# Opening the second matmul earlier, splitting its tiles in the first quads, and moving stores on a saturated TensorE

## The chip, the cores and the metric

The kernel runs on one core of one Trainium2 chip. The metric is the device time of one execution in microseconds (us), median of several runs. Before the change it was 341.34 us (three runs: 341.34, 342.12 and 340.13).

## What is computed

A forgetting attention (causal, with a decay from a cumulative sum of log f) over 8 batches, 8 heads, 576 positions and 64 dimensions is followed by a dense layer with SiLU, whose input row is the 8 heads' outputs side by side (512 wide), for 4608 rows:

```python
scores = scale * np.matmul(q, k.transpose(0, 1, 3, 2))
log_f = np.log(np.clip(f, 0.0001, 1.0))
cum = np.cumsum(log_f, axis=-1)
decay = cum[:, :, :, None] - cum[:, :, None, :]
scores = np.where(causal, -1000000000.0, scores + decay)
...
attn = attn / (np.sum(attn, axis=-1, keepdims=True) + 1e-09)
return np.matmul(attn, v).astype(np.float32)
...
x = np.ascontiguousarray(attn_out.transpose(0, 2, 1, 3)).reshape(B * S, H * D)
h = x @ w_in                          # 512 -> 2048
g = h * (1.0 / (1.0 + np.exp(-h)))
return (g @ w_out).astype(np.float32) # 2048 -> 512
```

## The kernel before

**The work.** The program is written out by hand; each engine and each DMA queue does its instructions in exactly the order in which the program lists them. Four kinds of TensorE work are interleaved.

- *Block 0 of each batch* (the first 128 positions of all heads): `turn0` (line 286, transposes q and k on TensorE, tile `tp`), `scores0` (line 318), `out0` (line 358, tile `dn`) and `back0` (line 391, transposes the result, tile `tx`; ScalarE copies it into the layer's input `x`, line 399). `two_more(b)` (line 857) does this for batches b and b+1, with pieces of the dense layer between the steps.
- *Units*: the other 448 positions of two heads are a unit n; four units are a batch, two units are a *quad* m, so there are 32 units and 16 quads (loop from line 960). For each unit `scores` (line 454) makes three pieces on TensorE, with the 64-row contraction of one head on each half of the array, and ScalarE takes the exponential (lines 474 and 480). `mask` and `mask_tail` (lines 484 and 490) zero the upper triangle on VectorE. `attend` (line 500) multiplies by the values (tile `dn`, lines 516 and 525) and VectorE divides (lines 533 and 534). `back(m)` (line 541) transposes a quad's result into `x`: for quads 0 to 2 and 15 on TensorE (tile `tx`, line 558, with VectorE's copies at lines 561 and 564), afterwards by DMA.
- *M1 chunks* (`m1_chunk`, line 570): 128 of the 2048 hidden columns for a group of rows (512, 256 or 384 wide), four matmuls into a tile `hp`; ScalarE makes `th` (line 585), VectorE makes `gt` (line 586).
- *M2 parts* (`m2_part`, line 604): a quarter of a 128-row output tile, four matmuls into `po`. After the fourth part ScalarE moves `po` to `osb` (line 632), and a store is put on a list. In quads 4 to 15 one M2 tile per quad is made in another way (`m2_rows`, line 639): the 128-row contraction is cut into halves of 64 rows that run side by side on the two halves of the array, 32 matmuls in each of two halves of the tile, into two tiles `pr`; VectorE moves them (`m2_fence`, `m2_out`, lines 657 and 661).

**The order.** `fill(us)` (line 748) lays down M1 chunks and M2 parts worth so many planned us; `step` (line 706) chooses between them; M2 may only run once `open2["w"]` is set (line 879, after the first `two_more` and a further `fill`). `whole` (line 913) finishes a started M2 tile and names the next whole one, if there is one. In a quad without a whole tile the order is the one from line 1004 on: pieces of the dense layer (`slot`) between the score pieces, then both `attend`. In a quad with one (line 981) the two halves of the M2 tile stand between the score pieces, and M1 chunks or M2 parts stand between the two `attend`.

**Buffers.** The PSUM tiles `tp`, `dn`, `tx`, `hp`, `po` and `pr` share four buffers (`pbig`, line 69); the score tiles have two of their own (`psc`, line 68). `osb` has four buffers (line 64), and `qkb`, the unit's q and k in bfloat16, has six (line 58).

**The supply.** SyncE's queue (SP) issues, in order: the loads of a unit's q (`qf`, line 167), of a batch's last positions (`qktf`, line 177) and of the values (`vf`, line 188), the DMA transposes of q and k (`qkT`, line 437), the stores (line 601) and the transposes of `back`. GpSimd (POOL) casts q (lines 410 and 414), issues the loads of k (line 158) and scales the values of a batch (`vp`, line 423, four instructions a batch). Unit n+3 is cast and transposed and unit n+4 is loaded in `turn(n)` (line 888); the values of batch 1 are loaded in `turn(2)` and `turn(3)` and needed first in unit 4, that is in quad 2. `store(n)` (line 598) issues the first n stores of the list; `slot` issues those that were on the list before it began.

Of the kernel before, what the change touches and what calls it, by code (L numbers as in the profile page):

```python
# [18 lines left out]
def kernel(  # L19
# [35 lines left out]

    const = ctx.enter_context(tc.tile_pool(name="const", bufs=1))
    stage = ctx.enter_context(tc.tile_pool(name="stage", bufs=1))
    conv = ctx.enter_context(tc.tile_pool(name="conv", bufs=6))
    qktp = ctx.enter_context(tc.tile_pool(name="qktp", bufs=4))
    upool = ctx.enter_context(tc.tile_pool(name="upool", bufs=4))  # L60
    recp = ctx.enter_context(tc.tile_pool(name="recp", bufs=2))
    xqp = ctx.enter_context(tc.tile_pool(name="xqp", bufs=2))
    tpool = ctx.enter_context(tc.tile_pool(name="tpool", bufs=3))
    opool = ctx.enter_context(tc.tile_pool(name="opool", bufs=4))
    xpool = ctx.enter_context(tc.tile_pool(name="xpool", bufs=1))
    setup_pool = tc.tile_pool(name="setup", bufs=1)
    setup = setup_pool.__enter__()
# [323 lines left out]
    def back0(b, *copies):  # L391
        xq = xqs.pop(b)[:, :, :].rearrange("p (c j) d -> p c (j d)", j=2)
        g, c0 = HEADS_OF[b]
        k = NCC // len(copies)
        for n, copy in enumerate(copies):
            tx = pbig.tile([P, k, P], BF16, name="tx", tag="big")
            for cc in range(k):
                nc.tensor.transpose(tx[:, cc, :], xq[:, n * k + cc, :], ident_bf[:, :])
            copy(out=xg(g)[:, n * k : (n + 1) * k, c0 : c0 + P], in_=tx[:, :, :])  # L399
# [100 lines left out]
    def attend(n):  # L500
        b, p = divmod(n, NP)
        if p % 2 == 0:
            xqs[n // 2] = xqp.tile([P, NGR, 2, D], BF16, name="xr", tag="xr", bufs=3)
        xq = xqs[n // 2]
        u, ut = us.pop(n), uts[n % 4]
        dn = pbig.tile([P, NGR, D + 1], FP32, name="dn", tag="big")

        def vals(kb, i):
            h = head(p, i)
            return v0[b][:, h, :] if kb == 0 else vbf[b][:, kb - 1, h, :]  # L510

        for i in range(2):
            for c in range(1, NM):
                for kb in range(c + 1):
                    o = AT[c, kb]
                    nc.tensor.matmul(  # L516
                        dn[:, i * NR + c - 1, :],
                        lhsT=u[:, i, o : o + P],
                        rhs=vals(kb, i),
                        start=(kb == 0),  # L520
                        stop=(kb == c),
                    )
        for i in range(2):
            for kb in range(NM + 1):
                nc.tensor.matmul(  # L525
                    dn[:, NGR - 1, :],
                    lhsT=ut[:, kb, i : i + 2, :].rearrange("p i t -> p (i t)"),
                    rhs=vals(kb, i),
                    start=(i == 0 and kb == 0),
                    stop=(i == 1 and kb == NM),  # L530
                )
        rec = recp.tile([P, NGR], FP32, name="rec", tag="rec")
        nc.vector.reciprocal(out=rec[:, :], in_=dn[:, :, D])
        nc.vector.tensor_tensor(  # L534
            out=xq[:, :, p % 2, :],
            in0=dn[:, :, 0:D],
            in1=rec[:, :, None].to_broadcast([P, NGR, D]),
            op=ALU.mult,
        )
# [166 lines left out]
    def step(force=0):  # L706

        a, c = at["m1"], at["m2"]
        want = wanted(a, c)
        if not want:  # L710
            return None
        g1 = M1[a][0] if a < len(M1) else NG
        g2 = M2[c][0] if c < len(M2) else NG
        can1 = g1 in ready and not (M1[a][1] == 0 and g1 > g2 + lag["g"])
        can2 = open2["w"] and c < len(M2) and g2 < g1
        kind = force if (force == 1 and can1) or (force == 2 and can2) else want
        if kind == 1:
            if M1[a][1] == 0:
                begin[g1] = (0, c)
            m1_chunk(g1, M1[a][1])  # L720
            at["m1"] += 1
            t = 4 * (GW[g1] / 2.4 + 2.5)
        else:
            m2_part(*M2[c])
            at["m2"] += 1
            t = 4 * (DM / 2.4 + 2.5)
        return t
# [20 lines left out]
    def fill(us_, least=0, ends=(0, 0)):  # L748

        left = us_ + at["left"]  # L750
        kinds = plan(left)
        kinds += [0] * (least - len(kinds))
        if any(ends) and kinds:
            if 2 not in kinds:
                kinds[0] = 2
            n1, n2 = len(kinds) - kinds.count(2), kinds.count(2)
            e0 = 1 if ends[0] else 0
            e1 = 1 if ends[1] and n2 > e0 else 0
            inner = n2 - e0 - e1
            n = n1 + inner  # L760
            mid = [2 if (x + 1) * inner // n > x * inner // n else 1 for x in range(n)]
            if inner and mid[-1] == 2 and e1 and not e0:
                mid = mid[::-1]
            kinds = [2] * e0 + mid + [2] * e1
        for k in kinds:
            t = step(k)
            if t is None:
                at["left"] = 0.0
                return
            left -= t / 1000  # L770
        at["left"] = left
# [85 lines left out]
    def two_more(b):  # L857
        for x in range(2):
            turn0(b + x, 0)
            turn0(b + x, 1)  # L860
        fill(1.2, 2)
        for x in range(2):
            scores0(b + x)
            mask0(b + x)
        fill(2.6 if b == 4 else 3.4, 3)
        out0(b)
        fill(0.6, 1)
        out0(b + 1)
        fill(0.8, 2)
        back0(b, on_act)  # L870
        fill(0.6, 1)
        back0(b + 1, on_act)
        fill(0.6, 1)

    fill(5.9)
    two_more(4)
    ready.add(1)
    fill(3.0)
    open2["w"] = True
    begin[M1[at["m1"]][0]] = (M1[at["m1"]][1], at["m2"])  # L880
    fill(6.0)
    two_more(6)
# [30 lines left out]
    def whole():  # L913

        while at["m2"] < len(M2) and M2[at["m2"]][2] and wanted(at["m1"], at["m2"]):
            t = step(2)
            at["left"] -= t / 1000
        c = at["m2"]
        while M1[at["m1"]][0] in ready and M1[at["m1"]][1] >= NFC - 4 and M2[c][0] == M1[at["m1"]][0]:
            at["left"] -= step(1) / 1000  # L920
        a = at["m1"]
        if c >= len(M2) or M2[c][2]:
            return None
        g1 = M1[a][0] if a < len(M1) else NG
        return M2[c][:2] if M2[c][0] < g1 else None
# [22 lines left out]
    def passed():  # L948
        for x in pending:
            x[0] -= 1  # L950
        while pending and pending[0][0] == 0:
            ready.update(pending.pop(0)[1])

    def slot(us_, least=0, ends=(0, 0)):
        n = len(stores)
        fill(us_, least, ends)
        store(n)
        passed()

    for m in range(NQ):  # L960
        n = 2 * m
        piece = 1.7 if m < 2 else 2.4
        if m == 2:
            assert at["m2"] >= M2_OF[0]
            first_pool.__exit__(None, None, None)
            gpools[0] = ctx.enter_context(tc.tile_pool(name="third", bufs=1))
            lag["g"] = 2
        if m == 4:
            lag["parts"] = 12
        goal = (spent() if m <= 4 else goal) + QUAD[m]  # L970
        rows = whole() if m > 0 and BY_DMA[m - 1] else None
        scores(n, 0)
        scores(n, 1)
        if m > 0:
            back(m - 1)
        turn(n)
        if m > 0:
            if m % 2 == 0:
                b = m // 2 - 1
                pending.append([2, [REST_OF[b]] + ([TAILS_OF[b][0]] if b == NM - 1 else [])])  # L980
        if rows:
            at["m2"] += 4
            m2_rows(*rows, 0)
            m2_fence(*rows)
            mask(n)
            scores(n, 2)
            scores(n + 1, 0)
            turn(n + 1)
            m2_rows(*rows, 1)
            mask_tail(n)  # L990
            mask(n + 1)
            scores(n + 1, 1)
            scores(n + 1, 2)
            m2_out(*rows)
            passed()
            attend(n)
            mask_tail(n + 1)
            slot(1.9, 3)
            attend(n + 1)
            slot(1.8)  # L1000
            rest(goal)
            at["left"] = 0.0
            continue
        slot(piece, 0, (1, 0))
        mask(n)
        scores(n, 2)
        scores(n + 1, 0)
        turn(n + 1)
        slot(piece, 0, (1, 0))
        mask_tail(n)  # L1010
        mask(n + 1)
        scores(n + 1, 1)
        scores(n + 1, 2)
        mask_tail(n + 1)
        slot(piece, 0, (1, 0))
        attend(n)
        attend(n + 1)
        slot(min(3.5, max(0.8, behind() - LAG)) if m > 1 else 0.8)
# [40 lines left out]
```

## Time and profile before

| What | Value |
|---|---|
| median of three runs | 341.34 us |
| the profiled execution, its own time | 340.98 us |
| its span, first to last instruction | 339.2 us |
| TensorE matmuls: `hp` line 577, 704 instructions | 122.1 us busy |
| `po` line 622, 400 instructions | 93.8 us busy |
| `pr` line 648, 768 instructions | 46.0 us busy |
| ScalarE: exponential of 128x1024 / `th` of 128x384 / `th` of 128x256, one | 1027 / 492 / 389 ns |
| VectorE: `gt` of 128x384 / `gt` of 128x256, one | 553 / 419 ns |
| VectorE: `osb` from `pr`, 128x256, one | 414 ns |
| DMA, mean over the span | 142 GB/s |

All times are microseconds from the start of the span unless marked ns. A busy TensorE is not TensorE at its peak: the profile models a matmul's end, so the time that a block of matmuls costs is read from the start of its first matmul to the start of the next block. A line of the timeline has the start, the time until the last instruction of the line ends, the engine, the line of code, the operation, the tiles and a count; in square brackets stands how long the engine was idle before it and what ended that.

Read from starts to starts in this way, four matmuls of an M2 part take 0.863 us, an M1 chunk 0.436 us (256 wide) or 0.650 us (384 wide), half an M2 tile in 64-row halves 1.75 us, and the attention product of one unit 0.85 us.

### The profile page before, as it was taken

The numbers are of one execution on the slowest core, as the hardware profiler recorded it, in microseconds if no ns is written. First come the engines' busy times: TensorE is split into PE (matmuls) and PEld (weight loads), VectorE is DVE, ScalarE is ACT, GpSimd is POOL, SyncE is SP. The second block draws the span as 40 slices with busy tenths as digits, with TensorE's granted clock in tenths as the row PEclk, the third lists the DMA queues.
The fourth block names the chain that finished last, engine by engine and source line by source line (L and its number), as shares of the span: only waits on it lengthen the run. The fifth ranks groups of instructions, "written<-read, shape, count | busy, mean of one in ns | idle before, by whom it ended". The sixth has DMA issues, their size and how long they took to land.

```text
span 339.2 us, 10025 instructions
## 1 busy us (share of the span) xinstructions
PE 330.6 (97%) x4132; PEld 222.4 (66%) x4132; DVE 193.6 (57%) x425; ACT 216.9 (64%) x389; POOL 137.4 (41%) x217
## 2 busy tenths in 40 slices
PE   7999899999999999999999999999999999999995
PEld 3745565577656768857766896867776676555654
DVE  4668935267567556655656865684672558334330
ACT  5766635677867767848748784875776485444431
POOL 8895417636756455454374434536060000000000
PEclk9999999999999999999999999999999999999999
DMA  8999999999999799999998969989763210001012
GB/s 151 190 185 222 182 210 155 199 236 177 156 190 236 117 215 134 163 211 151 168 178 172 142 130 175 134 168 165 148 123 66 56 37 33 31 33 64 33 62 63
DMA packets 144702, 48.00 MB, mean 142 GB/s; under 512 B 133328, under 2 KB 139728, under 8 KB 144656
## 3 DMA queue, kind: packets, MB, share of 16 engines
q1 hardware_dynamic: 115088, 36.60, 59.5%
q0 software_dynamic: 29408, 10.62, 26.6%
q8 instruction: 32, 0.52, 0.7%
q10 hardware_dynamic: 160, 0.13, 0.2%
q14 instruction: 14, 0.11, 0.1%
HBM read 36.85 MB, written 9.44 MB: 136 GB/s over the span
## 4 chain that ended last, share of the span: by engine, by line
PE 92%; ACT 2%; DVE 2%; DMA 2%; issue 1%; POOL 0%; POOLq 0%
PE hp L577 35%; PE po L622 24%; PE pr L648 12%; PE sc L469 7%; PE dn L516 6%; PE dn L525 3%; PE tp L294 2%; DMA qkb<-in_k_dram 2%; DVE u L344 1%; DVE gt L586 1%; ACT x L399 1%; PE sc L309 1%; PE sc L328 1%; ACT u L335 1%; PE tx L558 0%
## 5 line engine op out<-in xcount | busy, mean ns | idle before, releaser
L585 ACT ACTIVATE th<-hp 128x384 bf16<-128x384 f32 (+2 forms) x208 | 96.0, 469 | 78.7 <-PE hp L577 75.8
L586 DVE SCALAR_TENSOR_TENSOR gt<-th,hp 128x384 bf16<-128x384 bf16 (+2 forms) x208 | 107.1, 522 | 67.3 <-ACT th L585 58.5
L577 PE MATMUL hp<-x,w_in_bf 128*128 128x384 bf16 (+2 forms) x704 | 122.1, 321 | 1.5 <-ACT x L399 0.9
L577 PEld LDWEIGHTS <-w_in_bf 128*128 128x128 bf16 x832 | 79.4, 98 | 50.6 <-issue 1.8
L622 PE MATMUL po<-w_out_bf,gt 128*128 128x512 bf16 (+1 forms) x400 | 93.8, 371 | 0.0
L480 ACT ACTIVATE u<-sc 128x1024 bf16<-128x1024 f32 (+1 forms) x96 | 74.4, 814 | 6.4 <-PE sc L469 6.4
L622 PEld LDWEIGHTS <-gt 128*128 128x128 bf16 x400 | 37.6, 98 | 32.5 <-issue 0.2
L410 POOL CAST qkb<-qf 128x384 bf16<-128x384 f32 x32 | 16.7, 522 | 95.1 <-DMA qf<-in_q_dram 94.8
L648 PE MATMUL pr<-w_out_bf,gt 64*128 64x256 bf16 x768 | 46.0, 269 | 0.0
L158 POOL DMA_DIRECT2D qkb<-in_k_dram x56 | 43.8, 784 | 0.7 <-issue 0.7
L648 PEld LDWEIGHTS <-gt 64*128 64x128 bf16 x768 | 38.5, 94 | 2.8
L423 POOL TENSOR_TENSOR vp<-vf,w_bf 128x520 bf16<-128x520 f32 (+1 forms) x32 | 34.1, 1069 | 10.3 <-DMA vf<-in_v_dram 9.0
L632 ACT ACTIVATE osb<-po 128x512 f32<-128x512 f32 (+1 forms) x25 | 14.6, 583 | 22.6 <-PE po L622 19.5
L469 PE MATMUL sc<-qkT 64*128 64x128 bf16 (+1 forms) x640 | 27.9, 206 | 0.4 <-ACT u L480 0.3
L469 PEld LDWEIGHTS <-qkT 64*128 64x128 bf16 x640 | 19.9, 94 | 8.6 <-issue 6.5
L486 DVE TENSOR_TENSOR u<-u,tri 128x768 bf16<-128x768 bf16 x32 | 19.4, 605 | 10.5 <-ACT u L480 10.5
L474 ACT ACTIVATE ut<-sc 128x640 bf16<-128x640 f32 x32 | 22.5, 702 | 1.7 <-PE sc L469 1.3
L516 PEld LDWEIGHTS <-u 128*128 128x128 bf16 x576 | 20.6, 98 | 2.9
L516 PE MATMUL dn<-vp,u 128*128 128x65 bf16 x384 | 21.8, 194 | 0.0
L534 DVE TENSOR_TENSOR xr<-dn,rec 128x448 bf16<-128x448 f32 x32 | 20.0, 624 | 1.1
L516 PE MATMUL dn<-v,u 128*128 128x65 bf16 x192 | 20.0, 194 | 0.0
L577 PE MATMUL hp<-xt,w_in_bf 128*128 128x256 bf16 x128 | 16.6, 273 | 0.0
(72 smaller groups left out, 228.1 us busy)
## 6 DMA issues: line engine op xcount, KB each, us to landing
out_dram<-osb SPq DMA_DIRECT2D x32, 256.0 KB, 3.5
vf<-in_v_dram SPq DMA_DIRECT2D x26, 256.0 KB, 5.5
qf<-in_q_dram SPq DMA_DIRECT2D x64, 96.0 KB, 3.4
qkb<-in_k_dram POOLq DMA_DIRECT2D x56, 48.0 KB, 4.6
w_in_bf<-in_moe_w_in_dram POOLq DMA_DIRECT2D x4, 512.0 KB, 6.8
w_out_bf<-in_moe_w_out_dram POOLq DMA_DIRECT2D x4, 512.0 KB, 8.7
vf<-in_v_dram POOLq DMA_DIRECT2D x6, 256.0 KB, 10.3
qkb<-in_q_dram POOLq DMA_DIRECT2D x8, 128.0 KB, 5.5
```

Source lines behind the costliest of these rows:

```text
L158: nc.gpsimd.dma_start(out=t2[:, NR + 1 : NX, j * D : (j + 1) * D], in_=k[b, head(p, j), P:SM, :].rearrange("(c p) d -> p c d", p=P),)
L423: nc.gpsimd.tensor_tensor(out=vbf[b][r, c, :, :], in0=vst[b][c][r, :, :], in1=w_bf[r, c + 1, b * H : (b + 1) * H, None].to_broadcast([n, H ...
L469: nc.tensor.matmul(sc[:, i, o : o + q1 - q0], lhsT=kt, rhs=t[r, q0:q1], start=True, stop=True)
L474: nc.scalar.activation(out=ut[:, :, 0:3:2, :].rearrange("p k i t -> p i k t"), in_=sc[:, :, T0 : T0 + (NM + 1) * ST].rearrange("p i (k t) ...
L480: nc.scalar.activation(out=u[:, :, c * SM : c * SM + w], in_=sc[:, :, 0:w], func=ACT.Exp, scale=scale)
L516: nc.tensor.matmul(dn[:, i * NR + c - 1, :], lhsT=u[:, i, o : o + P], rhs=vals(kb, i), start=(kb == 0), stop=(kb == c),)
L534: nc.vector.tensor_tensor(out=xq[:, :, p % 2, :], in0=dn[:, :, 0:D], in1=rec[:, :, None].to_broadcast([P, NGR, D]), op=ALU.mult,)
L577: nc.tensor.matmul(hp[:, :], lhsT=w_in_bf[:, cc, fc * P : (fc + 1) * P], rhs=xcols(g, cc), start=(cc == 0), stop=(cc == NCC - 1),)
L585: nc.scalar.activation(out=th[:, :], in_=hp[:, :], func=ACT.Tanh, scale=0.5)
L586: nc.vector.scalar_tensor_tensor(out=gt[:, fc, :], in0=th[:, :], scalar=1.0, in1=hp[:, :], op0=ALU.add, op1=ALU.mult,)
L622: nc.tensor.matmul(po[:, :], lhsT=gt[:, fc, tb * P : (tb + 1) * P], rhs=w_out_bf[:, fc, m0:m1], start=(fc == 0), stop=(fc == NFC - 1),)
L648: nc.tensor.matmul(pos[g, tb][y], lhsT=gt[r, fc, tb * P : (tb + 1) * P], rhs=w_out_bf[r, fc, y * DM // 2 : (y + 1) * DM // 2], start=(half ...
```

## The change

Three things change, and the fill sizes around them.

1. M2 may run from the last `fill` of the first `two_more` on, one `fill` before what was there.
2. `whole()` is asked in every quad, so that quads 0, 1 and 2 run one M2 tile in 64-row halves (quad 3 finds no whole tile and keeps the old order). In quads 1 and 2 the transposes of `back(m - 1)` move from the head of the quad to behind the first `attend`. In quads 0 and 1 four M1 chunks stand between the two `attend` (`ones(4)`) and at least two behind them.
3. In quads 0 to 3 all stores on the list are issued at the head of the quad, ahead of the quad's loads on SP. `osb` gets a fifth buffer, and `qkb` gives up its sixth.

```diff
-    conv = ctx.enter_context(tc.tile_pool(name="conv", bufs=6))
+    conv = ctx.enter_context(tc.tile_pool(name="conv", bufs=5))
...
-    opool = ctx.enter_context(tc.tile_pool(name="opool", bufs=4))
+    opool = ctx.enter_context(tc.tile_pool(name="opool", bufs=5))
...
         back0(b + 1, on_act)
+        open2["w"] = True
         fill(0.6, 1)
...
     fill(3.0)
-    open2["w"] = True
...
+    def ones(k):
+        n = len(stores)
+        for _ in range(k):
+            step(1)
+        at["left"] = 0.0
+        store(n)
+        passed()
+
...
-        piece = 1.7 if m < 2 else 2.4
+        piece = 2.1 if m == 0 else 1.7 if m < 2 else 2.4
...
-        rows = whole() if m > 0 and BY_DMA[m - 1] else None
+        rows = whole()
+        late = bool(rows) and m > 0 and not BY_DMA[m - 1]
+        if m < 4:
+            store(len(stores))
         scores(n, 0)
         scores(n, 1)
-        if m > 0:
+        if m > 0 and not late:
             back(m - 1)
...
             mask_tail(n + 1)
-            slot(1.9, 3)
+            if late:
+                back(m - 1)
+            if m < 2:
+                ones(4)
+            else:
+                slot(1.9, 3)
             attend(n + 1)
+            if m < 4:
+                if m < 2:
+                    ones(2)
+                else:
+                    slot(min(5.3, max(0.8, behind() - LAG)))
+                continue
             slot(1.8)
```

The dense layer's work by quad, as the two programs list it (M1 chunks with their width, M2 parts, M2 tiles in halves):

| Quad | Before | After |
|---|---|---|
| ahead of quad 0 | 16 of 512, 16 of 256; 16 parts | the same |
| 0 | 6 of 256; 4 parts | 6 of 256; 1 tile in halves |
| 1 | 7 of 256; 3 parts | 10 of 256; 1 tile in halves |
| 2 | 3 of 256, 6 of 384; 6 parts | 5 of 384; 4 parts, 1 tile in halves |
| 3 | 10 of 384; 3 parts | 11 of 384; no M2 |
| 4 | 7 of 384; 4 parts, 1 tile in halves | 8 of 384; 4 parts, 1 tile in halves |

From quad 5 on a quad differs by a chunk or two, and the sums over the kernel are equal.

## Prediction

> **What bounds it now.** I read the busy shares and the chain first.
>
> ```profile
> PE 330.6 (97%) x4132; PEld 222.4 (66%) x4132; DVE 193.6 (57%) x425; ACT 216.9 (64%) x389; POOL 137.4 (41%) x217
> ...
> PEclk9999999999999999999999999999999999999999
> ...
> PE 92%; ACT 2%; DVE 2%; DMA 2%; issue 1%; POOL 0%; POOLq 0%
> ```
>
> TensorE is the bound, at full granted clock all through, and 92% of the chain is its own work. Both programs do the same M1 and M2 work, so the change can only win TensorE's waits and the cost of changing between 128-row and 64-row work, and can only lose by new waits. Its places are read in the timeline. First, the end of the first `two_more`:
>
> ```profile
> 37.09 0.39 PE L398 MATMUL tx<-ident_bf,xq 128*128 128x128 bf16 x4
> 37.29 0.60 ACT L585 ACTIVATE th<-hp 128x512 bf16<-128x512 f32 x1 [0.63 <-PE hp L577]
> 37.67 0.10 PEld L577 LDWEIGHTS <-w_in_bf 128*128 128x128 bf16 x1 [0.37 <-DVE gt L586]
> 37.78 0.58 ACT L399 COPY x<-tx 128x512 bf16<-128x512 bf16 x1
> 38.42 3.22 PE L577 MATMUL hp<-x,w_in_bf 128*128 128x256 bf16 x28 [0.94 <-ACT x L399]
> ```
>
> Four transposes cost 0.22 us elsewhere (57.64 to 57.86), so from 37.31 to 38.42 TensorE waits: until 37.67 for the buffer that `gt` frees, then for the copy into x. Second, a quad without M2 halves (quad 0) beside one with them (quad 4):
>
> ```profile
> 62.95 0.40 PE L469 MATMUL sc<-qkT 64*128 64x128 bf16 x8
> ...
> 65.53 0.40 PE L469 MATMUL sc<-qkT 64*128 64x128 bf16 x8 [0.25 <-ACT u L480]
> ...
> 69.98 0.19 PE L516 MATMUL dn<-v,u 128*128 128x65 bf16 x1
> ```
>
> ```profile
> 110.46 0.40 PE L469 MATMUL sc<-qkT 64*128 64x128 bf16 x8
> ...
> 110.91 1.91 PE L648 MATMUL pr<-w_out_bf,gt 64*128 64x256 bf16 x32
> ...
> 113.16 1.93 PE L648 MATMUL pr<-w_out_bf,gt 64*128 64x256 bf16 x32
> ...
> 115.44 0.20 PE L516 MATMUL dn<-v,u 128*128 128x65 bf16 x1
> ```
>
> Here the score pieces are what is left when the dense work is subtracted. Third, SP's queue and the values:
>
> ```profile
> 66.70 2.38 SPq L601 DMA_DIRECT2D out_dram<-osb  x4
> 69.13 1.57 SPq L167 DMA_DIRECT2D qf<-in_q_dram  x2
> 70.89 2.11 SPq L437 DMA_TRANSPOSE qkT<-qkb  x1
> ...
> 80.06 1.52 SPq L188 DMA_DIRECT2D vf<-in_v_dram  x2
> ```
>
> ```profile
> 86.67 2.38 POOL L423 TENSOR_TENSOR vp<-vf,w_bf 128x520 bf16<-128x520 f32 x2 [2.31 <-DMA vf<-in_v_dram]
> ```
>
> SP issues without a pause from 36 to 87 us, and the last values of batch 1 are scaled at 89.05; before, `attend` needs them at 92.06.
>
> **Part 1, M2 opened early: 0.72 us won.** In the new order an M2 part (0.863 us) stands ahead of the waiting chunk. It takes the buffer freed at 37.63, starts at about 37.70 and ends at 38.56; x has been ready since 38.37. So 0.863 us of work is done for a delay of 38.56 - 38.42 = 0.14. Bounds: 1.11 (the whole wait) and 0.2. What it uncovers: M2 now asks for w_out's quarters sooner. The third, issued at 32.35, lands 6.1 us later, at 38.4, and is wanted at 40.3; the last, issued at 33.16, lands 8.3 us later, at 41.5, and is wanted at 41.6 (38.56 + 3 x 0.436 + 2 x 0.863). The second `two_more` starts at 38.56 + 6 x 0.436 + 5 x 0.863 = 45.5 instead of 48.05, while its first q and k have landed by 43.1; `out0(6)` would run at 52.8 with its values scaled at 51.8 (54.96 before). All are covered, thinly; without cover each us late costs a us, which is the lower bound.
>
> **Part 2, M2 halves in quads 0 to 2: 1.36 us won.** From the first score to the first `dn`: quad 4 takes 4.98, less 2 x 1.75 = 1.48 of scores. Quad 0 takes 7.03, less 3 M2 parts (2.59) and 5 chunks (2.18): 2.26. Quad 1 (73.08 to 80.51): 7.43 less transposes 0.40, 3 parts 2.59, 6 chunks 2.62: 1.82. Quad 2 (82.86 to 92.06): 9.20 less 0.40, 5 parts 4.32, 3 chunks 1.31, 2 wide ones 1.30: 1.87. The surplus over 1.48 is 0.78 + 0.34 + 0.39 = 1.51; 0.43 of quad 0's is the wait for `u` shown above. A tile in halves costs 3.50 against 4 x 0.863 = 3.45, so 3 x 0.05 = 0.15 goes back. Bounds 0.9 (the wait in quad 0 stays) and 1.5. The tile's eviction goes from ScalarE (0.60) to VectorE (2 x 0.414 and a fence of 0.16), which has room in quads 0 and 2.
>
> By the Trainium skill, page "TensorE: Matmul & The Clock Gate", section "Measured speedup vs the span model", row packing stays below its ideal: four row tiles gave 3.07x. Estimated by that page a tile in halves would cost 3.45 x 4 / 3.07 = 4.5, three of them 3.0 us more than here, and the change would lose. The rows above show 1.75 us per half, so I keep 3.50.
>
> **Part 2, what it makes late: 0.2 us in quad 1.** The transposes of `back(0)` now stand behind the first `attend`, and VectorE's copies (0.56 + 0.21) behind `osb` and the division. From the start of the last score piece: division done at 2.3, `mask_tail` 2.5, copies 3.2. The four shared buffers then hold `tx` and three `hp`; the fourth chunk wants the buffer of `tx` at 3.1. Loss 0.1 to 0.2, I take 0.2; 0 if VectorE is a little faster, 0.7 if the masks run as long as the slowest in this profile (1.09 instead of 0.6). In quad 2 an M2 stretch of 2.6 us hides it.
>
> **Quad 3 is left without M2: 0.7 us lost.** M2's first 32 parts are used up by then, so quad 3 has eleven chunks and nothing else between scores. Spacing on the two other engines, where they are fed without pause:
>
> ```profile
> 106.73 1.32 ACT L585 ACTIVATE th<-hp 128x384 bf16<-128x384 f32 x3
> ...
> 107.30 1.48 DVE L586 SCALAR_TENSOR_TENSOR gt<-th,hp 128x384 bf16<-128x384 bf16 x3 [0.36 <-ACT th L585]
> ```
>
> A `th` every 0.41, a `gt` every 0.46, an exponential of 1024 every 0.91, a unit's last piece 0.85. From the quad's start TensorE lays the last four chunks ahead of `attend` at 6.1 to 8.7. ScalarE does `osb` 0.5, two exponentials to 2.4, two `th` to 3.15, last piece and exponential to 4.9, four `th` to 6.5, exponential and last piece to 8.25; only then the seventh `th` (0.49), and `gt` (0.55) frees the first buffer at 9.3 to 9.4. All four buffers hold `hp`, so `dn`, wanted at 8.7, waits 0.7. Bounds 0.2 and 1.2 (one `th` and `gt` either way). Quad 4 is M2-rich and does not carry it on.
>
> **Part 3, stores at the head: 0.5 us lost.** In quad 0 four stores (2.38 of issue) move ahead of the q load at 64.09. The `osb` they wait for is done at about 61.9, so SP does not stand still for them. But the load is issued at 66.5, and behind stores it lands in 5.5 us (the load at 69.13) rather than 3.3 (the one at 64.09): at 72.0 instead of 68.1. POOL's cast (0.85) waits for it, and SP's transpose for the cast: 72.9 instead of 70.89, with the loads of batch 1's values behind it on SP. 2.0 us of delay is one bound; the other is none, for the transposes of 2.11 and 2.43 took 1.26 where the queue was not backed up, and a drained queue makes that good. By quad: quad 0 starts at 62.95 - 0.72 = 62.23, quad 1 at 71.6 (1.48 + 3.50 + 0.85 + 1.74 + 0.85 + 0.87 + 0.10), quad 2 at 83.4, its first `attend` at 88.3, and it wants the last values at 89.0: just when they were ready before (89.05), because M1 and M2 now stand behind `attend` and not ahead of it. I take a quarter of the 2.0: 0.5 lost. The one store that moves in each of quads 1 to 3 takes 0.5 of SP's time ahead of the loads there instead of a little later; its `osb` is ready by then, and it is within the same bounds. The fifth `osb` buffer costs nothing: without it the tile of quad 0 (VectorE, at about 68) would wait for the first store. The sixth `qkb` buffer costs nothing either: the reused one was read by a transpose five units back.
>
> **Sum.** 0.72 + 1.36 - 0.2 - 0.7 - 0.5 = 0.68 won. The profiled execution took 340.98 (span 339.2 and 1.8 around it); 340.98 - 0.68 = 340.3. The median of the runs is 0.36 above it: 340.66, say 340.7. About 0.5%, 1.7 us, is what a measurement of this kernel can tell from no change, so this is no measurable change (0.45).
>
> **Rivals.** *The covers hold* (0.27): ScalarE and the supply keep up, nothing is lost; 341.34 - 2.08 = 339.3, faster. For it: ScalarE is busy 64% and quads 4 to 15 run the same pattern without waits. Against: quad 3 is not that pattern. *The values come late* (0.18): SP's delay is not made good and the landing slips too: 2.38 of issue and 2.2 of landing, 4.6 us on the path at quad 2's first `attend`, where nothing else is laid ahead: 341.34 - 1.18 + 4.6 = 344.8, slower. It decides from a delay of 1.2 on (no gain) and 2.9 (slower by 0.5%). For it: `vf` took 86.6 - 80.06 = 6.5 us to land here, and DMA is busiest here. Against: the issues ahead of those loads are the same in number. *M2 opens early to no effect* (0.10): the part waits for its buffer as long as the chunk waited for x; Part 1 falls away: 341.4.
>
> Forecast and last rival are both within 0.5%: same 0.55, faster 0.27, slower 0.18. Range: all losses high and part 1 low give 340.66 + 2.5 + 0.5 = 343.7, all losses nil 339.3, with part 1 whole 338.9; I take 339.0 to 343.5.
>
> **What would show it.** Right: an M2 part between 37.6 and 38.6 and an idle of under 0.1 ahead of the chunk; quads 0 to 2 with 1.48 of scores; in quad 3 an idle of about 0.7 ahead of the first `dn`, ended by `gt`; in quad 2 an idle ahead of `attend`, ended by POOL's `vp`, under 1 us. Wrong: no idle in quad 3 (339.6 or less), or one of several us in quad 2.

## The result, and the profile after

| | before | after |
|---|---|---|
| median of 22 runs each, in turn on one chip | 340.95 us | 341.97 us |
| ratio, with its 95% interval | | 1.0031 (1.002 to 1.0042) |
| span of the profiled execution | 339.2 us | 339.9 us |
| start of quad 0 / start of quad 4 | 62.95 / 110.46 | 63.15 / 111.31 |
| from quad 4 to the end of the span | 228.7 us | 228.6 us |

The kernel is 0.3% slower, about 1.0 us. That is within the 0.5% that the prediction called no measurable change, but on the other side of nought: 0.68 us were to be won. All of it arises before quad 4. The page of the changed kernel: busy shares, the slices of granted clock and of DMA, and the chain of waits.

```profile
PE 330.1 (97%) x4276; PEld 228.2 (67%) x4276; DVE 197.8 (58%) x434; ACT 216.5 (64%) x386; POOL 138.3 (41%) x217
...
PEclk9999999999999999999999999999999999999999
DMA  8999999999999699999998979969863110001012
...
PE 79%; DMA 10%; POOL 4%; issue 2%; DVE 2%; ACT 1%; SPq 1%; POOLq 0%
```

TensorE's clock and busy share are as before. What differs is the chain: 92% of it was TensorE's own work, now 79%, and DMA stands for 10% instead of 2%. The row of DMA shows why there is something to run into: 19 of its first 22 slices (187 us) are at 9 tenths, as many as before. The end now hangs on loads in several places; TensorE's timeline names them. First, the end of the first `two_more`:

```profile
36.96 0.39 PE L398 MATMUL tx<-ident_bf,xq 128*128 128x128 bf16 x4
37.53 1.02 PE L622 MATMUL po<-w_out_bf,gt 128*128 128x512 bf16 x4 [0.19 <-DVE gt L586]
38.40 0.60 PE L577 MATMUL hp<-x,w_in_bf 128*128 128x256 bf16 x4
...
40.99 0.60 PE L577 MATMUL hp<-x,w_in_bf 128*128 128x256 bf16 x4
42.42 1.02 PE L622 MATMUL po<-w_out_bf,gt 128*128 128x512 bf16 x4 [0.82 <-DMA w_out_bf<-in_moe_w_out_dram]
```

The M2 part starts at 37.53 and ends at 38.40, and the chunk after it waits for nothing. From the transposes to that chunk it is 1.44 instead of 1.33: 0.863 us of work is done for a delay of 0.11, about as worked out. Then the fourth part stands at 42.42 instead of 41.43 (40.99 + 0.436), waiting for the last quarter of w_out. From the start of the two chunks ahead of that place (33.60 before, 33.47 after) to quad 0 it took 29.35 before and 29.68 after: 0.33 lost where 0.72 was to be won. Quad 0, the halves of an M2 tile between the scores, in the same view:

```profile
63.15 0.40 PE L469 MATMUL sc<-qkT 64*128 64x128 bf16 x8
...
63.60 1.91 PE L648 MATMUL pr<-w_out_bf,gt 64*128 64x256 bf16 x32
...
65.80 1.93 PE L648 MATMUL pr<-w_out_bf,gt 64*128 64x256 bf16 x32
67.54 0.34 PE L469 MATMUL sc<-qkT,kT 64*128 64x384 bf16 x2
```

The first `dn` follows at 68.08: 4.93 from the first score, less two halves of 1.75, is 1.43 of scores. Quad 1 has the same 4.93, quad 2 has 1.40 of scores without its wait. Next the middle of quad 2, TensorE and then the queues of SP and GpSimd that feed it.

```profile
86.45 0.28 PE L469 MATMUL sc<-qkT 64*128 64x64 bf16 x8
87.36 0.40 PE L469 MATMUL sc<-qkT 64*128 64x128 bf16 x8 [0.63 <-DMA qkT<-qkb]
...
90.44 0.52 PE L525 MATMUL dn<-vp,ut 128*128 128x65 bf16 x4
```

```profile
65.13 2.34 SPq L601 DMA_DIRECT2D out_dram<-osb  x4
67.52 2.14 SPq L167 DMA_DIRECT2D qf<-in_q_dram  x2
...
75.87 0.53 SPq L601 DMA_DIRECT2D out_dram<-osb  x1
...
81.14 2.87 SPq L437 DMA_TRANSPOSE qkT<-qkb  x1
84.05 1.25 SPq L188 DMA_DIRECT2D vf<-in_v_dram  x2
```

```profile
88.34 2.38 POOL L423 TENSOR_TENSOR vp<-vf,w_bf 128x520 bf16<-128x520 f32 x2 [1.92 <-DMA vf<-in_v_dram]
```

The stores stand ahead of the q load, as designed. The transposes for unit 5, issued at 81.14, land at 87.31; its first score would have started at 86.58 and starts at 87.36, 0.78 later. Before, they landed at 84.53 for a use at 86.34. The last values of batch 1 are scaled at 90.72 (89.05 before) and hold up `dn` by another 0.24: the line of four matmuls lasts 0.52 instead of the 0.28 that the same line takes later. Last, quad 3:

```profile
105.17 2.77 PE L577 MATMUL hp<-x,w_in_bf 128*128 128x384 bf16 x16
108.86 0.19 PE L516 MATMUL dn<-v,u 128*128 128x65 bf16 x1 [0.92 <-DVE gt L586]
```

Four chunks of 0.650 take 2.60; from 105.17 to 108.86 are 3.69, so 1.09 of wait, and the releaser is `gt`, as predicted, for 0.7.

### The profile page after: what moved, and what is told of

Its sections match the earlier page's. It is cut to its first block, busy times and chain, and to the rows that moved or that the text cites. A ratio compares the mean times of both kernels' runs of the same rounds, so it can differ in the third digit from the quotient of the medians.

```text
span 339.9 us, 10326 instructions
## 1 busy us (share of the span) xinstructions
PE 330.1 (97%) x4276; PEld 228.2 (67%) x4276; DVE 197.8 (58%) x434; ACT 216.5 (64%) x386; POOL 138.3 (41%) x217
## 4 chain that ended last, share of the span: by engine, by line
PE 79%; DMA 10%; POOL 4%; issue 2%; DVE 2%; ACT 1%; SPq 1%; POOLq 0%
PE hp L577 29%; PE po L622 21%; PE pr L648 14%; PE sc L469 6%; PE dn L516 5%; DMA vf<-in_v_dram 4%; DMA w_out_bf<-in_moe_w_out_dram 3%; PE dn L525 3%; DMA qkb<-in_k_dram 2%; POOL v L349 2%; DMA qf<-in_q_dram 1%; DVE gt L586 1%; POOL w_in_bf L199 1%; PE tp L294 1%; POOL vp L423 1%
## 5 line engine op out<-in xcount | busy, mean ns | idle before, releaser
L622 PE MATMUL po<-w_out_bf,gt 128*128 128x512 bf16 (+1 forms) x352 | 81.7, 369 | 1.0 <-DMA w_out_bf<-in_moe_w_out_dram 0.8
L648 PE MATMUL pr<-w_out_bf,gt 64*128 64x256 bf16 x960 | 57.5, 269 | 0.0
L622 PEld LDWEIGHTS <-gt 128*128 128x128 bf16 x352 | 33.6, 98 | 29.6 <-issue 1.3
L648 PEld LDWEIGHTS <-gt 64*128 64x128 bf16 x960 | 48.0, 94 | 3.6
L632 ACT ACTIVATE osb<-po 128x512 f32<-128x512 f32 (+1 forms) x22 | 12.7, 578 | 26.8 <-PE po L622 26.8
L486 DVE TENSOR_TENSOR u<-u,tri 128x768 bf16<-128x768 bf16 x32 | 20.2, 631 | 12.2 <-ACT u L480 12.2
L659 DVE COPY fence<-pr 128x1 f32<-128x1 f32 x15 | 2.4, 158 | 26.2 <-PE pr L648 26.2
```

What stands on the lines that cost most here:

```text
L486: nc.vector.tensor_tensor(out=x, in0=x, in1=tri[:, None, None, :].to_broadcast([P, 2, NR, P]), op=ALU.mult)
L622: nc.tensor.matmul(po[:, :], lhsT=gt[:, fc, tb * P : (tb + 1) * P], rhs=w_out_bf[:, fc, m0:m1], start=(fc == 0), stop=(fc == NFC - 1),)
L648: nc.tensor.matmul(pos[g, tb][y], lhsT=gt[r, fc, tb * P : (tb + 1) * P], rhs=w_out_bf[r, fc, y * DM // 2 : (y + 1) * DM // 2], start=(half ...
```

## Experiments

Ratios are to the kernel before, measured in turn with it on one chip, with 95% intervals. The theory after the first reading was that each TensorE wait that was removed turned into another, for the supply or for the buffers.

**e1_wout_first.** The changed kernel, with the last two quarters of w_out ahead of two scalings on GpSimd that themselves wait for data:

```diff
-    convert_v0(4)
-    convert_v0(5)
     load_w_out(2)
     load_w_out(3)
+    convert_v0(4)
+    convert_v0(5)
```

> The changed kernel with w_out's last two quarter loads issued ahead of the two value conversions that stood before them on POOL. Theory (three new waits, found in the trace after): the chunk at 40.99 waits about 1.0 us because the fourth M2 part wants the last quarter, which lands at 42.38. Issued at about 26 instead of 32 to 33 it lands before 41, the wait goes, and the time falls by 0.7 to 1.0 us against the changed kernel, to about the kernel before (ratio to before 1.000). Rival 1: that wait is hidden behind a later one (the supply of quad 2, which does not move): quad 2 waits that much longer and the time stays (1.003). Rival 2: the halves of the first three quads themselves cost the time: also 1.003, with the wait gone and no longer wait in quad 2.

Ratio 1.0003 (0.9982 to 1.0023). The quarters are issued from 26.1 to 27.6, the last lands at 40.42 and nothing waits for it; quad 0 starts 28.93 after the two chunks of above (29.35 before, 29.68 in the changed kernel). The waits further on stay: 0.85 for unit 5, 0.56 for the values, 0.71 ahead of quad 3's `dn`. So w_out cost the changed kernel about 0.75 (by the traces) to 1.0 us (by the medians; the two intervals touch).

**e2_no_head_stores.** The changed kernel without `if m < 4: store(len(stores))`.

> The changed kernel without the stores at the head of quads 0 to 3 (they come at the slots, behind the loads of units 4 and 5). Theory: the four stores made the load and the transpose of units 3 to 5 and the values of batch 1 late by 1.5 to 2.5 us; without them the two waits in quad 2 (0.78 for the transposed q and k of unit 5, 0.24 for the values) go and the time falls by 0.8 to 1.0 us (ratio to before about 1.000). Rival: the same bytes and issues stand ahead of those loads either way and quad 2 simply asks earlier than the kernel before did; the two waits stay within 0.3 us of where they are, ratio 1.002 to 1.003.

Ratio 1.0036 (1.0018 to 1.0054), not to be told from the changed kernel. The wait for unit 5 doubles to 1.66, which neither expectation had. SP's queue shows the reason:

```profile
73.87 3.35 SPq L601 DMA_DIRECT2D out_dram<-osb  x5
...
81.91 3.56 SPq L437 DMA_TRANSPOSE qkT<-qkb  x1
```

The five stores now go out later, between unit 4's transposes and unit 5's, which land at 88.58. That the stores stand at the head is not what makes them costly. Its time says little: in the profiled execution TensorE was idle for 2.3 in two waits for w_out, against 0.82 in the changed kernel.

**e3_open_late.** The changed kernel with M2 opened at its old place.

> The changed kernel with M2 opened where it was before. Theory: part 1 won 0.72 at the copy into x and lost 1.0 at the last quarter of w_out, so undoing it gives 0.2 to 0.3 back at the start of quad 0 (about 62.95 again); the supply of quad 2 does not depend on it: within 0.3 us of the changed kernel, ratio 1.002 to 1.003. Rival (part 1 is a plain win, the loss is all later): 0.7 us slower than the changed kernel, ratio 1.005.

Ratio 1.0045 (1.0017 to 1.0073). The wait for x (0.9 idle) is back, the one for w_out is gone; 0.55 for unit 5 and 0.7 in quad 3 remain. The two readings disagree: the ratio is nearer to the rival's 1.005 than to the theory's 1.002 to 1.003, but in the profile e3 took 77.02 from the two chunks to quad 4, the changed kernel 77.84, and e3 lost 1.0 later, in quad 10. What the early opening is worth in the changed kernel stays open.

**e4_no_split.** The changed kernel with halves only from quad 4 on (`rows = whole() if m > 0 and BY_DMA[m - 1] else None`).

> The changed kernel with whole tiles only from quad 4 on, so without halves in quads 0 to 2 (early M2, head stores and buffers stay). Theory: the halves win 1.36 in the score pieces, but put quad 2's need for unit 5 and the values 3 to 4 us earlier relative to the supply (1.0 lost) and leave quad 3 without M2 (1.1 lost): undoing them wins 0.5 to 0.9 against the changed kernel, ratio 1.000 to 1.002, with no wait in quads 2 and 3 and 1.8 to 1.9 us of scores in quads 1 and 2. Rival (the halves are a plain win and the loss is the stores' and w_out's): slower than the changed kernel by 1.0 to 1.4, ratio 1.006 to 1.007.

Ratio 0.9995 (0.9973 to 1.0018). Quad 3 has no wait, w_out costs 0.6, and unit 5 costs 0.41, where no wait was expected. From the two chunks to quad 4 it took 76.70, 1.14 less than the changed kernel. So the halves, meant to win 1.36 between the scores, are a loss of about 1.2 us as the change places them: they bring the demand on unit 5 forward and take M2 out of quad 3.

**e7_hold_stores.** e1 with the first six stores held until quad 1 has issued its loads, with a sixth buffer for `osb` and one less for `qkb`:

```diff
+    held = {"on": True}
...
-        n = max(n, 0)
+        n = 0 if held["on"] else max(n, 0)
...
+            if m == 1:
+                held["on"] = False
+                store(len(stores))
```

> The kernel of e1_wout_first, with the first six stores held on the list until quad 1 has issued unit 6's loads and transposes and the last values of batch 1; osb gets a sixth buffer, qkb gives up one. Theory (the early supply is late because SP's queue and the DMA engines carry the stores too, 1.5 MB ahead of unit 5's transposes): unit 5's transposed q and k land 2 us or more earlier than in e1 (86.5), at 84.5 or before, TensorE's waits of 0.85 ahead of unit 5's first scores and 0.56 ahead of the values of batch 1 vanish, ratio to before 0.9960 to 0.9975. Rival (the chain load, cast, transpose sets the landing, each step with its own latency, and stores only fill gaps): unit 5 lands within 0.7 of 86.5, waits stay over 0.8 together, ratio 0.9995 to 1.0010. Second rival (the cost only moves): quad 2 has no wait but quad 3 or 4 gains one for the transposes of units 6 to 8, behind the six stores, ratio 0.999 to 1.000.

Ratio 0.9951 (0.9927 to 0.9974). Unit 5's transposes land at 83.86, 2.7 earlier than in e1, and quad 2 has no wait at all; 0.7 remains in quad 3. Quads 0 to 3 take 46.79 (48.17 in e1, 47.51 before). SP's queue:

```profile
77.43 1.55 SPq L437 DMA_TRANSPOSE qkT<-qkb  x1
79.03 2.94 SPq L188 DMA_DIRECT2D vf<-in_v_dram  x2
...
84.97 3.75 SPq L603 DMA_DIRECT2D out_dram<-osb  x6
```

The theory's supply part is shown: it was the stores among the loads, not their place at the head. In e7 and in e9 (below), which hold the stores, unit 5 lands 0.64 and 1.03 after the start of quad 2; in the eight profiles with halves in quad 2 and stores among the loads it is 2.39 to 4.03.

**e8_q3_tile and e8b_q3_tile_again.** e1 with the dense work of quads 2 to 4 shared out so that quad 3 has a whole M2 tile:

```diff
-        late = bool(rows) and m > 0 and not BY_DMA[m - 1]
+        late = bool(rows) and m > 0 and not BY_DMA[m - 1] and m != 2
...
-                pending.append([2, [REST_OF[b]] + ([TAILS_OF[b][0]] if b == NM - 1 else [])])
+                pending.append([1 if m == 2 else 2, [REST_OF[b]] + ([TAILS_OF[b][0]] if b == NM - 1 else [])])
...
-            if m < 2:
+            if m < 4:
                 ones(4)
...
-                if m < 2:
-                    ones(2)
-                else:
-                    slot(min(5.3, max(0.8, behind() - LAG)))
+                ones((2, 2, 5, 3)[m])
```

> The kernel of e1_wout_first, with the dense work of quads 2 to 4 shared out again so that quad 3 too has a whole M2 tile to run in 64-row halves: fewer M1 chunks in quad 3, the M2 parts of quad 4 drawn forward. Theory (quad 3 stalls because without M2 all four shared buffers hold chunks that wait for ScalarE and VectorE): the wait ahead of the first dn of quad 3 (0.7 in e1, 1.1 in the changed kernel) falls under 0.2, quad 3's scores take 1.5 instead of about 1.9, ratio to before 0.9970 to 0.9985. Rival (the two engines have a backlog from the chunks that they have to work off in any order): the wait moves to quad 2 or 4 with the chunks, ratio 0.9995 to 1.0010. The waits of quad 2 for unit 5 (0.85 and 0.56) stay in both.

> The kernel of e8_q3_tile, unchanged, for a second interval: the theory stands if its ratio is again 0.9925 to 0.9965. Quad 0 began 1.3 us later there than in e1_wout_first, at 63.6, and unit 5's transposes landed 0.06 ahead of their use: if quad 0 begins nearer to 62.3 here, a wait of 0.3 to 1.2 for unit 5 stands in quad 2 and the span is the same within 0.5, since the supply sets when quad 2 can go on; if TensorE's own work set it, the span would be shorter by that 1.3.

Ratios 0.9942 (0.9923 to 0.9961), better than expected, and 0.9968 (0.9949 to 0.9987), just outside the 0.9925 to 0.9965 that were asked for; medians 339.0 and 340.0. Quad 3 of the first:

```profile
102.26 0.34 PE L469 MATMUL sc<-qkT,kT 64*128 64x384 bf16 x2
...
104.03 2.76 PE L577 MATMUL hp<-x,w_in_bf 128*128 128x384 bf16 x16
...
107.50 2.11 PE L577 MATMUL hp<-x,w_in_bf 128*128 128x384 bf16 x12
```

The first `dn` stands at 102.79, 0.53 after the last score piece, and the four chunks take 2.61 (104.03 to the next `dn` at 106.64): no wait. Quads 0 to 3 take 45.90 in both executions, 2.27 less than in e1, more than quad 3's wait and scores: quad 2's waits are gone too. There the transposes of `back(1)` now stand at the head, so that unit 5 is wanted 0.6 later; its q and k landed 0.06 and 0.62 ahead of their use. So the expectation that quad 2's waits stay did not hold; nor did the repeat's, which began quad 0 at 62.55 and yet had no wait for unit 5; its span was not shorter, for a reason in quad 10 (below).

**e9_hold_and_q3.** The edits of both.

> The edits of e7_hold_stores and e8_q3_tile together. Theory (the two waits are independent, one in quad 2 from the supply, one in quad 3 from the buffers): the gains add, 2.0 to 2.4 us off e1, ratio to before 0.9930 to 0.9955, faster than both kernels. Rival (one wait covers for the other: what TensorE gains in quad 2 it waits for the next unit's q and k in quad 3 or 4): no better than the better of the two alone, 0.9965 or above, with a wait for unit 6 or 7 in the trace.

Ratio 0.9965 (0.994 to 0.9989): no gain over either. Quads 0 to 3 take 46.17, without a wait for units 6 or 7, so the rival's reason is not seen either; 0.6 went to w_out, whose last quarter landed at 42.00, and 1.2 to quad 10.

**b0_before_again.** The kernel before, once more.

> The kernel before, unchanged, for a second trace of it. If the landing of w_out's last quarter varies from execution to execution by as much as it moved between the two kernels (41.49 before, 42.38 after), it lands here outside 41.2 to 41.8; if it is tied to what was issued ahead of it, which is the same in both kernels, it lands within that. No wait for it either way, since TensorE wants it at 44 or later here; unit 5's transposed q and k land at 84 to 85, 1.5 us or more ahead of their use.

The last quarter of w_out, issued at 32.70, landed at 42.01, 9.3 us later; in the first profile, issued at 33.16, at 41.49, 8.3 us later. In the profiles with this order of issues (before twice, the changed kernel, e2, e3, e4, e10) it landed between 41.49 and 43.15. It varies with the execution, and the first profile's landing is the earliest of the seven, and its 8.3 the shortest way from issue to landing (8.9 to 9.8 in the others). Unit 5 landed at 84.36, 1.4 ahead of its use, where 1.5 or more was expected.

**e12_early_wout.** The kernel before with M2 opened early and w_out moved as in e1; no halves before quad 4, no stores at the head.

> The kernel before with M2 opened early and the last two quarters of w_out ahead of the values of batches 4 and 5; no halves in quads 0 to 2, no stores at the head. Here unit 5's transposes have 1.8 us in hand and quad 3 has M2 parts. Rival (the first step of the prediction, right once w_out comes in time): 0.72 us faster, ratio 0.9970 to 0.9985, quad 0 begins at 62.2 and quad 4 0.7 earlier than before. Theory (anything won early is met by the supply only where the slack of 1.8 is used up, which it is not here): the same 0.72. They part in what follows for the change: if the gain is not there, the step was wrong by itself; if it is, it was lost by the halves using up the same slack.

Ratio 0.9980 (0.9966 to 0.9995): 0.68 us, with an interval of 0.2 to 1.2. Part 1 of the change alone, with its load in time, is a gain. The trace doesn't show the whole of it where Part 1 acts:

```profile
37.40 0.38 PE L398 MATMUL tx<-ident_bf,xq 128*128 128x128 bf16 x4 [0.41 <-DVE gt L586]
37.62 1.03 PE L622 MATMUL po<-w_out_bf,gt 128*128 128x512 bf16 x4
38.48 0.60 PE L577 MATMUL hp<-x,w_in_bf 128*128 128x256 bf16 x4
```

The part starts in time and the chunk waits for nothing, but the transposes ahead of them now wait for a buffer, as they do in e1 and wherever w_out was moved: the part costs a delay of 0.33 instead of 0.11, which leaves 0.53 of the 0.75 won in the changed kernel. Why they wait was not tried. Quad 0 began at 60.52, not 62.2, since two chunks and one part more lie behind it; from the two chunks to quad 4, with the same work, it took 76.50 (76.86 and 76.74 in the two profiles of before), a gain of 0.24 to 0.36. The rest of the difference between the spans lies elsewhere, most of it behind quad 4, where the order of the dense work differs too. Unit 5's slack shrank to 0.50.

**e11_q3_open_late.** e8 with M2 opened at its old place.

> The kernel of e8_q3_tile with M2 opened at its old place, after the last fill. Theory (before quad 2 the supply sets the pace, so the 0.72 us that the early opening wins on TensorE come back as a wait): within 0.2 us of e8, ratio 0.993 to 0.997, with the wait of about 1.1 for x back and no wait for unit 5 in quad 2. Rival (the early opening is worth its 0.72 once w_out comes in time): 0.7 us above e8, ratio 0.9955 to 0.9985.

Ratio 0.9940 (0.992 to 0.996), no worse than e8: the medians give the early opening nothing there. The trace doesn't agree with the theory's reason: the wait for x is back (0.7 idle) and quad 2 waits 0.5 for the values, and from the two chunks to quad 4 e11 took 76.53 where e8 took 74.63 and 74.83. Each profile of e8 lost this again elsewhere: the first began the two chunks at 34.91, 1.9 later than e11 (33.00), and the repeat waited 2.1 in quad 10, where e11 and the first had no wait. Whether that holds for their other runs, and so why e8 is not faster than e11 by the medians, is open.

**e10_pool_order.** In quad 3 of the changed kernel VectorE had done this, and GpSimd beside it:

```profile
106.39 0.39 DVE L492 TENSOR_TENSOR ut<-ut,trit 128x128 bf16<-128x128 bf16 x1
106.70 0.64 DVE L486 TENSOR_TENSOR u<-u,tri 128x768 bf16<-128x768 bf16 x1
107.27 1.07 DVE L492 TENSOR_TENSOR ut<-ut,trit 128x128 bf16<-128x128 bf16 x1
108.27 1.93 DVE L586 SCALAR_TENSOR_TENSOR gt<-th,hp 128x384 bf16<-128x384 bf16 x4
```

```profile
106.20 0.50 POOL L410 CAST qkb<-qf 128x384 bf16<-128x384 f32 x1 [4.97 <-DMA qf<-in_q_dram]
106.64 0.29 POOL L414 CAST qkb<-qktf 128x128 bf16<-128x128 f32 x1
106.88 1.58 POOL L158 DMA_DIRECT2D qkb<-in_k_dram  x2
```

The second mask lasts 1.07 and the `gt` that frees the buffer starts after it. The edit moves GpSimd's loads and scalings ahead of its cast:

```diff
+        if n == 7:
+            prepare(n)
         if n < NU - 3:
             cast_qk(n + 3)
-        prepare(n)
+        if n != 7:
+            prepare(n)
```

> The changed kernel with one order changed: in the turn of unit 7 (quad 3) GpSimd issues the load of unit 11's k and scales the last two values of batch 2 before it casts unit 10, and not after. In the changed kernel the second mask_tail of quad 3 took 1.07 us beside these loads, 0.23 where GpSimd is idle. Theory (VectorE's mask stands still while GpSimd works, and that made 0.4 of the 1.1 that the first dn waited; the rest is ScalarE's, which is what was predicted): that mask_tail takes 0.25 or less, the block of four chunks ahead of the dn takes 3.2 to 3.3 instead of 3.69 (2.60 without a wait). Rival (ScalarE and the four buffers set all of it): the mask is short and the block still takes 3.6 or more. Other rival (the mask's length has nothing to do with GpSimd): the mask takes 0.8 or more again. The total moves by 0.4 at most, which one look cannot tell.

VectorE's line at that place, and GpSimd's next work:

```profile
108.38 0.23 DVE L492 TENSOR_TENSOR ut<-ut,trit 128x128 bf16<-128x128 bf16 x1
109.04 1.95 DVE L586 SCALAR_TENSOR_TENSOR gt<-th,hp 128x384 bf16<-128x384 bf16 x4 [0.43 <-ACT th L585]
```

```profile
108.84 0.50 POOL L410 CAST qkb<-qf 128x384 bf16<-128x384 f32 x1 [2.38 <-DMA qf<-in_q_dram]
```

The mask takes 0.23, `gt` now waits for ScalarE's `th`, and the block ahead of `dn` takes 3.31 (106.34 to 109.65): 0.7 of wait. Three profiles with the old order agree: in e1, e3 and e7 this mask took 0.30, 0.30 and 0.22, and the idle time ahead of `dn` was 0.53, as in e10; it was 0.74 in e2, whose mask took 0.95, and 0.92 in the changed kernel. So quad 3's 1.09 is 0.7 of ScalarE, the predicted term, and 0.4 of a stretched mask. Since the mask was short in three executions without the edit, e10 doesn't show that the new order keeps it short. The one run took 342.54; w_out's last quarter landed at 43.15 in it and cost 2.6 idle in two waits.

## Why the prediction was wrong

Gains are negative here.

| Step | Predicted | Profile of the changed kernel |
|---|---|---|
| M2 opened early: the wait for x | -0.72 | -0.75, the part at 37.53, no idle ahead of the chunk |
| its cover, w_out | 0 | +0.99 |
| halves in quads 0 to 2 | -1.36 | -1.54: 1.43, 1.43 and 1.40 of scores, 1.48 foreseen |
| copies of `tx` in quad 1 | +0.2 | +0.17, four chunks in 1.91 instead of 1.74 |
| supply in quad 2 | +0.5 | +1.02: 0.78 unit 5, 0.24 values |
| quad 3 without M2 | +0.7 | +1.09 |
| sum | -0.68 | +0.98 |

From the two chunks to quad 4 the two profiles took 76.86 and 77.84: the same 0.98. Their spans differ by 0.73 alone, since the changed kernel began the chunks 0.13 earlier and took 0.12 less behind quad 4; the medians differ by 1.02.

*The step that failed* is the cover under Part 1, which stands in the sum at nothing and cost 0.99: w_out's last quarter "lands 8.3 us later, at 41.5, and is wanted at 41.6", "All are covered, thinly; without cover each us late costs a us". The want was right (41.43). The landing was one execution's, and the earliest of seven: in others it came up to 1.7 us later from the same order of issues, and a margin of 0.1 was costed at nothing. The bounds named it, but the likeliest value should have been the middle of what a landing can do, not the one that was seen. e1 takes this wait away and the ratio falls from 1.0031 to 1.0003; e12 shows that the early opening is a gain where the load comes in time (0.68 by the medians, less in the trace). The cover and the two terms below, mis-sized by 0.52 and 0.39, make 1.90 together; the other terms came out 0.24 better than forecast, and so 0.68 that were to be won became 0.98 lost.

*The supply in quad 2* was mis-sized, 1.02 for 0.5, and sought in the wrong transfer. The prediction followed the values to POOL's `vp`, and set quad 2's first `attend` against them. The q and k of unit 5, on the same queue and one instruction earlier, had 1.81 us in hand before and were not set against their use; they were late first, and the values after them a little. e7 shows the cause to be the stores among the loads. The prediction's account of Part 3 (stores moved to the head delay the loads) was wrong in this: without them at the head (e2) unit 5 is later still, in the one profile there is.

*Quad 3* was right in place, releaser and mechanism, and 0.4 too small: its working follows ScalarE and has no term for VectorE's masks, which stand ahead of `gt`. The prediction had a slow mask in its hands for quad 1 only, and took 1.09 for the slowest where the profile of before has one of 1.20. e8 removes the wait by giving the quad M2 work.

*Right* were the part at 37.5, the scores between halves, the price of a tile in halves (two of 1.75), the `tx` copies, and that quad 4 carries nothing on. The signs of being right, named in advance, nearly all appeared and none of those of being wrong did: they watched the places that had been priced, and none watched the landing of w_out.

Of the rivals, "the covers hold" is not what this change did, but about what e8 reaches: 339.0 and 340.0 against the 339.3 given. "The values come late" had the direction and, with 4.6, several times the size. What beats both kernels, with intervals that lie below 1, are e7, e8, e9, e11 and e12, all with w_out ahead of waiting work on GpSimd's queue. The lowest ratios, 0.994, are those of e8's first set of runs and of e11, which also keep the halves and leave an M2 tile for quad 3; they do not stand clear of e7's 0.9951.

## What to carry to other kernels

A wait that TensorE loses comes back at the next thing that it asks for sooner: list for every load between the edit and the end its landing and its use, before and shifted, and charge each whose slack is smaller than the shift plus the spread of its landing, not only the one that looks latest. One profile gives one draw of a landing in a loaded queue; here the same load varied by 1.7 us and the one draw was the earliest of seven, so a margin of 0.1 is no margin. And a queue's order matters twice: loads that stand behind an instruction which itself waits (w_out behind two scalings), and bulk writes that go out just ahead of the load that is short.

## What the runs showed of the hardware

**Masks stretched beside GpSimd's work.** In the changed kernel `mask` took at most 0.56 in all 16 cases, and `mask_tail` at most 0.23 in all 15, in which no GpSimd instruction overlapped; where one was running at the start they went up to 1.36 and 1.60, though some kept their length. `gt`, which reads one operand from PSUM, stayed under 0.70 in all 208. In quad 10 of the repeat of e8, VectorE and then GpSimd:

```profile
202.84 2.63 DVE L492 TENSOR_TENSOR ut<-ut,trit 128x128 bf16<-128x128 bf16 x1
205.39 1.93 DVE L586 SCALAR_TENSOR_TENSOR gt<-th,hp 128x256 bf16<-128x256 bf16 x5
```

```profile
201.72 1.56 POOL L158 DMA_DIRECT2D qkb<-in_k_dram  x2
203.31 2.07 POOL L423 TENSOR_TENSOR vp<-vf,w_bf 128x520 bf16<-128x520 f32 x2
```

```profile
205.85 0.60 PE L577 MATMUL hp<-xt,w_in_bf 128*128 128x256 bf16 x4 [2.08 <-DVE gt L586]
```

A mask of 0.23 lasts 2.63, until the last of three GpSimd instructions has ended (205.38), and TensorE stands idle for 2.08 meanwhile, its buffers full. That quad took 14.97 or 14.98 in six profiles with this schedule and 17.22 here; 15.8 to 16.2 in e3, e7 and e9. The Trainium skill, page "SBUF — State Buffer", section "SBUF: two separate sides", says that VectorE and GpSimd share a pair of ports under an exclusive lock, which an operation with two SBUF inputs needs against a GpSimd operation that reads SBUF, and that the loser blocks for the whole instruction. The traces agree beside the scalings, and show that VectorE can lose several times in a row. Beside issues of loads alone, which the sentence does not name, 9 of 11 masks in the changed kernel kept their length, but the one of quad 3 took 1.07; what decides that is not shown. Whether the masks' collisions account for the spread of these kernels' times (338.7 to 342.2 for that one) was not tried.

**Landings in a loaded queue.** A quarter of w_out (512 KB) took 6.1 to 11.0 us from issue to landing in the profiles of the kernel before, the changed kernel, e2 and e10. The same page, section "The DMA setup-cost knee", fits 2 us and the bytes at 436 GB/s, an estimate of 3.2 us by that page for a transfer alone; no run here had one alone. SP's issue of one unit's transposes took 1.22 at the least and up to 4.27 (in e4).
